# Attention units woven matmul by matmul into the second product of a fused attention and MLP kernel, and the last unit's values moved into the next tile's first blocks

## The chip, the cores and the metric

The kernel runs on one core of one Trainium2 chip. The metric is the device time of one execution in microseconds (us); lower is better. TensorE (PE in the profile) does the matmuls and transposes, VectorE (DVE) and ScalarE (ACT) the element-wise work, GpSimd (POOL) and SyncE (SP) start the transfers.

## The reference

Eight batches of eight heads, 576 positions, head size 64, go through attention with a sliding window of 32 positions to either side. The result, 4608 tokens of 512 features, goes through two matrix products with a tanh-approximated Gelu between them. Inputs and output are float32.

```python
scores = scale * np.matmul(q, k.transpose(0, 1, 3, 2))        # scale = 1/sqrt(64)
mask = np.abs(pos[:, None] - pos[None, :]) <= 32
scores = np.where(mask, scores, -1e9)
attn = softmax(scores)                                        # max taken off, exp, sum
x = (attn @ v).transpose(0, 2, 1, 3).reshape(4608, 512)
h = x @ w_in                                                  # w_in 512 x 2048
g = 0.5 * h * (1 + tanh(sqrt(2/pi) * (h + 0.044715 * h**3)))
out = g @ w_out                                               # w_out 2048 x 512
```

## The kernel before

Everything on TensorE is done in fp16 with float32 accumulation. The tokens of a batch are ordered so that a batch is 576 neighbouring columns of one large tile in SBUF, `xT`, which has the features on the partitions: four groups of 128 features, and group number pr holds the heads 2pr and 2pr+1. The two products work on nine tiles of 512 tokens. Tile t needs columns 512t to 512t+511, so it needs batches up to t, and the attention of batch t+1 is computed while tile t goes through its products. Batch 0 is computed ahead of all tiles (the prologue). Tiles 0 to 6 carry the attention of batches 1 to 7; tiles 7 and 8 carry none.

The first product of tile t, in `ffn_in`, makes 16 blocks of 128 hidden features, each of four accumulating matmuls (`dc` 0 to 3, one for each group of features of `xT`), followed by the Gelu on ACT, which writes into the tile `gT`. The second product, in `ffn_out`, makes four blocks of 128 tokens, each of 16 accumulating matmuls, followed by a copy (`yo`) on DVE and the transfers out. Both kinds of block take their accumulator from one ring of three PSUM buffers (`psM`): a new block has to wait until the block three places earlier has been emptied by its Gelu or its copy.

Attention of a batch comes in eight units: four pairs of heads (pr), two halves of the sequence each. For a unit, `scores` issues six matmuls into the PSUM tile `ps_s`, then an exponential on ACT (`pe`, line 204) and a multiplication with the 0/1 mask on DVE (`pm`, line 206). `values` issues twelve matmuls into `ps_od`, which give the weighted values and the row sums, then a logarithm and an exponential of its negative on ACT (`lt`, line 231, and `rt`, line 233: together the reciprocal of the sums), and a multiplication on DVE that writes the normalised result into `xT` (line 234, "normalisation" below). `ps_s` and `ps_od` have one buffer each. So scores u+1 have to wait for the exponential of unit u, and values u+1 for the normalisation of unit u.

Ahead of the units, q and k have to be cast to fp16 on DVE and transposed on TensorE into `QT` and `KT`: `cast_tail` and `trans_tail` for the last 64 positions of all heads, `cast_pair` and `trans_pair` for the rest of each pair. This is done between the blocks of the first product of tile t for batch t+1. The transposes all go through one PSUM buffer. The loads of q and k for batch t+2 are issued on SP at the start of tile t, behind the output transfers of tile t-1; the loads of v are issued on POOL.

The order is written out by hand: each engine runs its instructions in the order in which the program issues them. In the second product, TensorE's 64 matmuls were cut into 16 runs of four (`ffn_out(t, t4, f0, f1)`), and a table `sched` says which unit calls stand ahead of which run: scores u ahead of run 3u/2 (rounded down), values u two runs later. Ahead of this, `load_exp_table` switches ACT's function table from Gelu to logarithm and exponential; the switch back to Gelu stands ahead of the first Gelu of the next tile.

Of the kernel before, what the change touches and what calls it, by code (L numbers as in the profile page):

```python
# [9 lines left out]
FP32 = mybir.dt.float32  # L10
FP16 = mybir.dt.float16
AF = mybir.ActivationFunctionType
# [12 lines left out]
    1: [(2, 72, 104), (3, 88, 136), (4, 120, 144)],  # L25
}
SW = 416


@with_exitstack  # L30
def kernel(
# [9 lines left out]
    nc = tc.nc  # L41
# [4 lines left out]
    NF = DF // 128  # L46
# [7 lines left out]
    def load_exp_table():  # L54
        nc.scalar.add_instruction(mybir.InstLoadActFuncSet(  # L55
            name=nc.get_next_instruction_name(), act_func_set_id=exp_set, ins=[], outs=[]))
# [8 lines left out]
    psM = ctx.enter_context(tc.tile_pool(name="psM", bufs=3, space=PSUM))  # L65
# [9 lines left out]
    ones = const.tile([128, 64], FP16, name="ones")  # L75
    masks = [const.tile([128, SW], FP16, name=f"mask{h}") for h in range(2)]
    KTs = [const.tile([128, NPAIR, 640], FP16, name=f"KT{i}") for i in range(2)]
    Vs = [const.tile([128, 5, H, 64], FP16, name=f"V{i}") for i in range(2)]
    w_in16 = big.tile([128, 4, DF], FP16, name="w_in16")
    w_out16 = big.tile([128, NF, DM], FP16, name="w_out16")  # L80
# [4 lines left out]
    def load_qk(b, split):  # L85
        qr = rawp.tile([128, H, 256], FP32, name="qr")
        kr = rawp.tile([128, H, 256], FP32, name="kr")
        tr = rawp.tile([128, H, 64], FP32, name="tr")
        raws[b] = (qr, kr, tr)
        step = H // split  # L90
        for h0 in range(0, H, step):
            for src, dst in ((q, qr), (k, kr)):
                nc.sync.dma_start(
                    dst[:, h0:h0 + step, :],
                    src[b, h0:h0 + step, 0:512, :].rearrange("h (p j) d -> p h (j d)", j=4))
            if h0 == 0:
                nc.sync.dma_start(tr[0:64, :, :], q[b, :, 512:576, :].rearrange("h s d -> s h d"))
                nc.sync.dma_start(tr[64:128, :, :], k[b, :, 512:576, :].rearrange("h s d -> s h d"))

    def load_v(b):  # L100
        V = Vs[b % 2]
        for c in range(4):
            nc.gpsimd.dma_start(V[:, c, :, :],  # L103
                                v[b, :, 128 * c:128 * c + 128, :].rearrange("h p d -> p h d"))
        nc.gpsimd.dma_start(V[0:64, 4, :, :], v[b, :, 512:576, :].rearrange("h p d -> p h d"))
# [11 lines left out]
    for h in range(2):  # L117
# [3 lines left out]
        for (c, p0, p1) in PIECES[h]:  # L121
# [11 lines left out]
            off += 4 * n  # L133
        assert off == SW
    for i in range(4):
# [12 lines left out]
    def cast_tail(b):  # L148
        t16 = hp.tile([128, H, 64], FP16, name="t16")
        nc.vector.tensor_copy(t16, raws[b][2])  # L150
        halfs[b] = t16
        QTs[b] = ap_.tile([128, NPAIR, 4, NP_], FP16, name="QT")

    def trans_tail(b):
        t16 = halfs[b]
        pt = psT.tile([128, NPAIR, 128], FP16, name="pt", tag="T", padded_shape=[128, 8, 128])
        for pr in range(NPAIR):
            nc.tensor.transpose(pt[:, pr, :], t16[:, 2 * pr:2 * pr + 2, :], idn)
        for pr in range(NPAIR):
            nc.vector.tensor_copy(  # L160
                QTs[b][:, pr, :, 128:144],
                pt[:, pr, 0:64].rearrange("d (p j) -> d j p", j=4))
        nc.vector.tensor_copy(KTs[b % 2][:, :, 512:576], pt[:, :, 64:128])

    def cast_pair(b, pr):
        qr, kr, tr = raws[b]
        q16 = ap_.tile([128, 4, 2, 64], FP16, name="q16")
        k16 = ap_.tile([128, 4, 2, 64], FP16, name="k16")
        for src, dst in ((qr, q16), (kr, k16)):
            nc.vector.tensor_copy(  # L170
                dst.rearrange("p j h d -> p h j d"),
                src[:, 2 * pr:2 * pr + 2, :].rearrange("p h (j d) -> p h j d", j=4))
        halfs[(b, pr)] = (q16, k16)
# [15 lines left out]
    def scores(b, u):  # L189
# [3 lines left out]
        for (c, p0, p1) in PIECES[hf]:  # L193
# [8 lines left out]
            off += 4 * n  # L202
        pe = ap_.tile([128, 2, SW], FP16, name="pe")
        nc.scalar.activation(pe, ps[:, :, 0:SW], AF.Exp, scale=SCALE)  # L204
        pm = ap_.tile([128, 2, SW], FP16, name="pm")
        nc.vector.tensor_tensor(  # L206
            pm, pe, masks[hf].rearrange("p (o w) -> p o w", o=1).broadcast_to([128, 2, SW]),
            op=ALU.mult)
        units[(b, u)] = pm

    def values(b, u):
        pr, hf = u // 2, u % 2
        pm = units.pop((b, u))
        V = Vs[b % 2]
        od = psO.tile([128, 2, 512], FP32, name="ps_od")
        off = 0
        last = len(PIECES[hf]) - 1
        for i, (c, p0, p1) in enumerate(PIECES[hf]):
            n = p1 - p0
            a, e = p0 - HALF * hf, p1 - HALF * hf  # L220
            for w in range(2):
                for h in range(2):
                    r0 = 64 * h
                    nc.tensor.matmul(  # L224
                        od[r0:r0 + 64, w, 0:4 * HALF].rearrange("d (j p) -> d j p", j=4)[:, :, a:e],
                        V[:, c, 2 * pr + h, :] if w == 0 else ones,
                        pm[:, h, off:off + 4 * n].rearrange("k (j p) -> k j p", j=4),
                        start=(i == 0), stop=(i == last), skip_group_check=True)
            off += 4 * n
        lt = ap_.tile([128, 4 * HALF], FP32, name="lt")  # L230
        nc.scalar.activation(lt, od[:, 1, 0:4 * HALF], AF.Ln)  # L231
        rt = ap_.tile([128, 4 * HALF], FP32, name="rt")
        nc.scalar.activation(rt, lt, AF.Exp, scale=-1.0)  # L233
        nc.vector.tensor_tensor(  # L234
            xT[:, pr, b * S:(b + 1) * S].rearrange("d (j p) -> d j p", j=4)[:, :, HALF * hf:HALF * hf + HALF],
            od[:, 0, 0:4 * HALF].rearrange("d (j p) -> d j p", j=4),
            rt.rearrange("d (j p) -> d j p", j=4), op=ALU.mult)


    gTs = {}  # L240

    def ffn_in(t, fc):
        if fc == 0:
            gTs[t] = gp.tile([128, NF, 512], FP16, name="gT")
        ph = psM.tile([128, 512], FP32, name="ph", tag="mm")
        for dc in range(4):
            nc.tensor.matmul(ph, w_in16[:, dc, fc * 128:fc * 128 + 128],  # L247
                             xT[:, dc, t * 512:(t + 1) * 512],
                             start=(dc == 0), stop=(dc == 3))
        nc.scalar.activation(gTs[t][:, fc, :], ph, AF.Gelu_apprx_tanh)  # L250

    out_v = out.rearrange("(b p j) f -> b j p f", b=B, j=4)
    pys = {}

    def ffn_out(t, t4, f0, f1):
        if f0 == 0:
            pys[t4] = psM.tile([128, 512], FP32, name="py", tag="mm")
        py = pys[t4]
        for fc in range(f0, f1):
            nc.tensor.matmul(py, gTs[t][:, fc, t4 * 128:t4 * 128 + 128], w_out16[:, fc, :],  # L260
                             start=(fc == 0), stop=(fc == NF - 1))
        if f1 == NF:
            yo = yp.tile([128, 512], FP32, name="yo")
            nc.vector.tensor_copy(yo, py)  # L264
            g = t * 512 + t4 * 128
            end = g + 128
            m = 0
            while g < end:
                seg = g // NP_
                e = min(end, (seg + 1) * NP_)  # L270
                p0 = g - seg * NP_
                nc.sync.dma_start(out_v[seg // 4, seg % 4, p0:p0 + e - g, :], yo[m:m + e - g, :])
                m += e - g
                g = e
# [12 lines left out]
    values(0, 7)  # L287


    for t in range(NT):  # L290
        b = t + 1
        att = b < B
        if att and b + 1 < B:
            load_qk(b + 1, 1)
            load_v(b + 1) if b + 1 >= 2 else None
        for fc in range(NF):
            if att:
                if fc == 1:
                    cast_tail(b)
                    cast_pair(b, 0)  # L300
                if fc == 2:
                    trans_tail(b)
                if fc in (4, 7, 10, 13):
                    pr = (fc - 4) // 3
                    trans_pair(b, pr)
                    if pr < 3:
                        cast_pair(b, pr + 1)
            ffn_in(t, fc)
        sched = {}
        if att:  # L310
            load_exp_table()
            for u in range(8):
                sched.setdefault((3 * u) // 2, []).append((scores, u))
                sched.setdefault((3 * u) // 2 + 2, []).append((values, u))
        for i in range(16):
            for fn, u in sched.get(i, []):
                fn(b, u)
            ffn_out(t, i // 4, 4 * (i % 4), 4 * (i % 4) + 4)


# [28 lines left out]
```

## Time and profile before

| | us |
|---|---|
| median of 3 runs | 402.92 (402.8 to 403.68) |
| the profiled execution | 404.22 |
| its span, first to last instruction | 402.5 |
| TensorE busy in it | 337.8 (84%) |
| ACT busy | 213.5 (53%) |
| DVE busy | 156.7 (39%) |
| one stage with attention (second product of a tile, first product of the next) | 42.75 |
| mean granted clock of TensorE | 0.998 of full speed |

In a row of the timeline stand the start and the duration in us, the engine, the source line, the operation, output and inputs by the program's names, the number of instructions, and in brackets how long the engine had been idle before and what ended that. Matmuls overlap in the array, and their ends are modelled, so the distance from one group's start to the next group's start is what a group costs TensorE, and not its duration. A row of the view by stretches has the stretch, its length, then for TensorE, its weight loads, DVE, ACT and POOL the busy time with the number of instructions, then the granted clock, the share of the transfer engines and GB/s. In the table of waits stand the total in us, the number of waits and the longest.

### The profile page before, as it was taken

The page shows a single profiled execution, that of the slowest core. Times are in us where ns is not written, and L with a number is a line of the kernel's source. Part 1 is how long each engine was busy: PE and PEld are TensorE (multiplying, and loading weights), DVE is VectorE, ACT ScalarE, POOL GpSimd, SP SyncE. Part 2 cuts the span into 40 slices and gives each one's busy share as a digit, 9 for nine tenths or more (in the row PEclk, how much of TensorE's full clock was granted, in tenths as well). Part 3 has the DMA queues.
Part 4 walks back from the last instruction along what each step waited for, and adds up shares of the span by engine and source line. Part 5 has one row for each costly group of instructions (what it writes and reads, how often), then busy time and mean ns, then how long its engine had stood idle before and what let it go on. Part 6 is the DMA issues. An engine that isn't in the chain of part 4 may idle for free.

```text
span 402.5 us, 6406 instructions
## 1 busy us (share of the span) xinstructions
PE 337.8 (84%) x2592; PEld 171.4 (43%) x2592; DVE 156.7 (39%) x347; ACT 213.5 (53%) x352; POOL 45.0 (11%) x67
## 2 busy tenths in 40 slices
PE   0454997899789988898889978997899888999995
PEld 0343453445344534454444534453445344444442
DVE  3545443445244524453454434452445244002011
ACT  1254566555755565646555665557555656530710
POOL 9512120040004000400012000400000000000000
PEclk9999999999999999999999999999999999999999
DMA  9999990197029900594019501980110001002102
GB/s 173 265 238 215 252 156 20 36 137 210 2 52 82 267 1 29 66 207 100 28 31 209 135 12 43 126 221 0 54 30 24 2 26 55 26 5 76 28 26 78
DMA packets 72574, 37.64 MB, mean 94 GB/s; under 512 B 47456, under 2 KB 67936, under 8 KB 72544
## 3 DMA queue, kind: packets, MB, share of 16 engines
q1 hardware_dynamic: 30816, 28.32, 25.6%
q0 software_dynamic: 41728, 8.92, 24.5%
q8 instruction: 20, 0.33, 0.4%
q14 instruction: 10, 0.08, 0.1%
HBM read 36.70 MB, written 9.44 MB: 115 GB/s over the span
## 4 chain that ended last, share of the span: by engine, by line
PE 67%; ACT 19%; DVE 6%; issue 4%; POOL 3%; ACTq 0%; POOLq 0%
PE ph L247 31%; PE py L260 20%; PE ps_od L224 9%; ACT pe L204 7%; ACT lt L231 6%; DVE xT L234 4%; ACT rt L233 4%; PE ps_s L197 3%; ACT L55 2%; PE pt L179 2%; PE pt L181 2%; POOL V L103 1%; POOL w_in L116 1%; POOL mask L125 1%; POOL mask L127 0%
## 5 line engine op out<-in xcount | busy, mean ns | idle before, releaser
L260 PE MATMUL py<-w_out,gT 128*128 128x512 f16 x576 | 140.4, 381 | 0.0
L247 PE MATMUL ph<-xT,w_in 128*128 128x512 f16 x576 | 133.6, 383 | 0.1
L250 ACT ACTIVATE gT<-ph 128x512 f16<-128x512 f32 x144 | 86.0, 597 | 80.8 <-PE ph L247 80.8
L247 PEld LDWEIGHTS <-w_in 128*128 128x128 f16 x576 | 55.2, 99 | 60.9 <-issue 2.2
L204 ACT ACTIVATE pe<-ps_s 128x832 f16<-128x832 f32 x64 | 54.8, 857 | 35.2 <-PE ps_s L197 35.1
L260 PEld LDWEIGHTS <-gT 128*128 128x128 f16 x576 | 48.8, 97 | 54.4
L206 DVE TENSOR_TENSOR pm<-pe,mask 128x832 f16<-128x832 f16 x64 | 37.9, 592 | 59.6 <-ACT pe L204 58.2
L234 DVE TENSOR_TENSOR xT<-ps_od,rt 128x288 f16<-128x288 f32 x64 | 29.3, 458 | 66.4 <-ACT rt L233 66.4
L231 ACT ACTIVATE lt<-ps_od 128x288 f32<-128x288 f32 x64 | 26.2, 410 | 52.3 <-PE ps_od L224 52.3
L103 POOL DMA_DIRECT2D V<-in_v_dram x32 | 28.6, 901 | 204.3 <-PE ps_od L224 178.5
L224 PE MATMUL ps_od<-pm,V 128*64 128x192 f16 (+4 forms) x384 | 35.7, 240 | 18.1 <-DVE xT L234 17.9
L264 DVE COPY yo<-py 128x512 f32<-128x512 f32 x36 | 24.7, 686 | 65.0 <-PE py L260 65.0
L197 PE MATMUL ps_s<-QT,KT 64*128 64x192 f16 (+4 forms) x384 | 24.2, 233 | 25.8 <-ACT pe L204 22.0
L224 PEld LDWEIGHTS <-V 128*64 128x64 f16 x384 | 26.1, 115 | 42.3 <-issue 42.2
L224 PE MATMUL ps_od<-pm,ones 128*64 128x192 f16 (+4 forms) x384 | 33.4, 236 | 0.0
L197 PEld LDWEIGHTS <-KT 64*128 64x128 f16 x384 | 14.8, 97 | 42.8 <-issue 36.6
L182 DVE COPY QT<-pt 128x512 f16<-128x512 f16 x32 | 13.6, 425 | 40.7 <-PE pt L181 40.7
L233 ACT ACTIVATE rt<-lt 128x288 f32<-128x288 f32 x64 | 28.3, 442 | 2.0
L179 PE MATMUL pt<-idn,q 128*128 128x128 f16 x128 | 13.3, 230 | 15.4 <-DVE q L170 15.4
L224 PEld LDWEIGHTS <-ones 128*64 128x64 f16 x384 | 25.1, 116 | 0.0
L183 DVE COPY KT<-pt 128x512 f16<-128x512 f16 x32 | 21.8, 681 | 0.0
L179 PEld LDWEIGHTS <-q 128*128 128x128 f16 x128 | 10.0, 102 | 22.4 <-DVE q L170 15.8
(27 smaller groups left out, 106.9 us busy)
## 6 DMA issues: line engine op xcount, KB each, us to landing
qr<-in_q_dram SPq DMA_DIRECT2D x7, 1024.0 KB, 7.3
kr<-in_k_dram SPq DMA_DIRECT2D x7, 1024.0 KB, 10.6
V<-in_v_dram POOLq DMA_DIRECT2D x32, 128.0 KB, 5.2
w_in<-in_moe_w_in_dram POOLq DMA_DIRECT2D x4, 512.0 KB, 22.3
w_out<-in_moe_w_out_dram POOLq DMA_DIRECT2D x4, 512.0 KB, 29.4
out_dram<-yo SPq DMA_DIRECT2D x8, 256.0 KB, 2.4
out_dram<-yo SPq DMA_DIRECT2D x8, 224.0 KB, 2.4
out_dram<-yo SPq DMA_DIRECT2D x8, 192.0 KB, 3.2
```

The source lines that it names most:

```text
L103: nc.gpsimd.dma_start(V[:, c, :, :], v[b, :, 128 * c:128 * c + 128, :].rearrange("h p d -> p h d"))
L179: nc.tensor.transpose(pt[:, j, :], q16[:, j, :, :], idn)
L197: nc.tensor.matmul(ps[:, h, off:off + 4 * n].rearrange("k (j p) -> k j p", j=4), KTs[b % 2][r0:r0 + 64, pr, 128 * c:128 * c + 128], QTs[b] ...
L204: nc.scalar.activation(pe, ps[:, :, 0:SW], AF.Exp, scale=SCALE)
L206: nc.vector.tensor_tensor(pm, pe, masks[hf].rearrange("p (o w) -> p o w", o=1).broadcast_to([128, 2, SW]), op=ALU.mult)
L224: nc.tensor.matmul(od[r0:r0 + 64, w, 0:4 * HALF].rearrange("d (j p) -> d j p", j=4)[:, :, a:e], V[:, c, 2 * pr + h, :] if w == 0 else ones ...
L231: nc.scalar.activation(lt, od[:, 1, 0:4 * HALF], AF.Ln)
L233: nc.scalar.activation(rt, lt, AF.Exp, scale=-1.0)
L234: nc.vector.tensor_tensor(xT[:, pr, b * S:(b + 1) * S].rearrange("d (j p) -> d j p", j=4)[:, :, HALF * hf:HALF * hf + HALF], od[:, 0, 0:4 ...
L247: nc.tensor.matmul(ph, w_in16[:, dc, fc * 128:fc * 128 + 128], xT[:, dc, t * 512:(t + 1) * 512], start=(dc == 0), stop=(dc == 3))
L250: nc.scalar.activation(gTs[t][:, fc, :], ph, AF.Gelu_apprx_tanh)
L260: nc.tensor.matmul(py, gTs[t][:, fc, t4 * 128:t4 * 128 + 128], w_out16[:, fc, :], start=(fc == 0), stop=(fc == NF - 1))
```

## The change

`ffn_out` now issues one matmul, and the second product is a loop over 64 of them. The unit calls have positions in this loop, counted in matmuls: scores 0 ahead of matmul 0, scores u ahead of matmul 15 + 7(u-1) for u from 1 to 7, values u ahead of matmul 19 + 7u for u from 0 to 6. So scores 7 stand ahead of matmul 57, and values 6 ahead of matmul 61. Values u now come behind scores u+1.

Values 7 stand behind the 64th matmul. `ffn_in` can issue part of a block (`d0` to `d1`), and the first three blocks of the next tile are begun here with their first three matmuls, which read the groups of features 0 to 2 of `xT`: block 0 ahead of values 7, blocks 1 and 2 behind them. Group 3 is what units 6 and 7 write. The next tile's loop begins with the three fourth matmuls and their Gelus, and goes on with block 3. All three buffers of the ring are held by these blocks until their Gelus.

The casts and transposes of q and k move by one or two blocks: the tail's casts and transposes and the first pair's cast to block 3 (from blocks 1 and 2), the transposes of the pairs to blocks 5, 8, 11 and 14 (from 4, 7, 10 and 13).

```diff
--- before.py
+++ after.py
@@ -25,6 +25,10 @@
     1: [(2, 72, 104), (3, 88, 136), (4, 120, 144)],
 }
 SW = 416
+
+
+
+FIRST, LAG, STEP = 15, 4, 7
 
 
 @with_exitstack
@@ -238,28 +242,32 @@
 
 
     gTs = {}
-
-    def ffn_in(t, fc):
-        if fc == 0:
+    phs = {}
+
+    def ffn_in(t, fc, d0=0, d1=4):
+        if fc == 0 and d0 == 0:
             gTs[t] = gp.tile([128, NF, 512], FP16, name="gT")
-        ph = psM.tile([128, 512], FP32, name="ph", tag="mm")
-        for dc in range(4):
+        if d0 == 0:
+            phs[fc] = psM.tile([128, 512], FP32, name="ph", tag="mm")
+        ph = phs[fc]
+        for dc in range(d0, d1):
             nc.tensor.matmul(ph, w_in16[:, dc, fc * 128:fc * 128 + 128],
                              xT[:, dc, t * 512:(t + 1) * 512],
                              start=(dc == 0), stop=(dc == 3))
-        nc.scalar.activation(gTs[t][:, fc, :], ph, AF.Gelu_apprx_tanh)
+        if d1 == 4:
+            nc.scalar.activation(gTs[t][:, fc, :], ph, AF.Gelu_apprx_tanh)
 
     out_v = out.rearrange("(b p j) f -> b j p f", b=B, j=4)
     pys = {}
 
-    def ffn_out(t, t4, f0, f1):
-        if f0 == 0:
+    def ffn_out(t, i):
+        t4, fc = i // NF, i % NF
+        if fc == 0:
             pys[t4] = psM.tile([128, 512], FP32, name="py", tag="mm")
         py = pys[t4]
-        for fc in range(f0, f1):
-            nc.tensor.matmul(py, gTs[t][:, fc, t4 * 128:t4 * 128 + 128], w_out16[:, fc, :],
-                             start=(fc == 0), stop=(fc == NF - 1))
-        if f1 == NF:
+        nc.tensor.matmul(py, gTs[t][:, fc, t4 * 128:t4 * 128 + 128], w_out16[:, fc, :],
+                         start=(fc == 0), stop=(fc == NF - 1))
+        if fc == NF - 1:
             yo = yp.tile([128, 512], FP32, name="yo")
             nc.vector.tensor_copy(yo, py)
             g = t * 512 + t4 * 128
@@ -287,35 +295,51 @@
     values(0, 7)
 
 
+    begun = False
     for t in range(NT):
         b = t + 1
         att = b < B
         if att and b + 1 < B:
             load_qk(b + 1, 1)
             load_v(b + 1) if b + 1 >= 2 else None
-        for fc in range(NF):
+        if begun:
+
+            for fc in range(3):
+                ffn_in(t, fc, 3, 4)
+        for fc in range(3 if begun else 0, NF):
             if att:
-                if fc == 1:
+                if fc == 3:
                     cast_tail(b)
                     cast_pair(b, 0)
-                if fc == 2:
                     trans_tail(b)
-                if fc in (4, 7, 10, 13):
-                    pr = (fc - 4) // 3
+                if fc in (5, 8, 11, 14):
+                    pr = (fc - 5) // 3
                     trans_pair(b, pr)
                     if pr < 3:
                         cast_pair(b, pr + 1)
             ffn_in(t, fc)
-        sched = {}
         if att:
             load_exp_table()
+            at = {0: [(scores, 0)]}
             for u in range(8):
-                sched.setdefault((3 * u) // 2, []).append((scores, u))
-                sched.setdefault((3 * u) // 2 + 2, []).append((values, u))
-        for i in range(16):
-            for fn, u in sched.get(i, []):
-                fn(b, u)
-            ffn_out(t, i // 4, 4 * (i % 4), 4 * (i % 4) + 4)
+                if u:
+                    at.setdefault(FIRST + STEP * (u - 1), []).append((scores, u))
+                if u < 7:
+                    at.setdefault(FIRST + LAG + STEP * u, []).append((values, u))
+            for i in range(64):
+                for fn, u in at.pop(i, []):
+                    fn(b, u)
+                ffn_out(t, i)
+            assert not at
+            ffn_in(t + 1, 0, 0, 3)
+            values(b, 7)
+            ffn_in(t + 1, 1, 0, 3)
+            ffn_in(t + 1, 2, 0, 3)
+            begun = True
+        else:
+            for i in range(64):
+                ffn_out(t, i)
+            begun = False
 
 
 # ---- launch: one core; inputs and outputs as the reference has them ----
```

## The prediction

> **What bounds the kernel now.** I read the page first (span, engines), then the table of waits, then one tile's stage in the view by stretches and the timeline. Page and waits (us in total, times, longest):
>
> ```profile
> span 402.5 us, 6406 instructions
> PE 337.8 (84%) x2592; PEld 171.4 (43%) x2592; DVE 156.7 (39%) x347; ACT 213.5 (53%) x352; POOL 45.0 (11%) x67
> ...
> PE ps_s L197 <- ACT pe L204: 22.0, 29, 1.6
> PE ps_od L224 <- DVE xT L234: 17.9, 32, 1.5
> ```
>
> TensorE is the busiest engine, and its large waits are both in the attention units: the next scores wait for the exponential to empty their only score tile, the next values for the normalisation to empty their only output tile. Two stretches of one stage (tile 3: second product with attention, then the first product of tile 4; columns are length, then busy time by engine):
>
> ```profile
> 187.70:214.53 26.83, 21.82 (x209) 10.91 (x209) 10.20 (x19) 16.55 (x27) 4.21 (x5) 1.00 0.28 41
> 214.53:230.45 15.92, 15.92 (x101) 8.19 (x100) 8.61 (x23) 8.96 (x15) 0.00 (x0) 1.00 0.88 185
> ```
>
> The first product keeps TensorE busy for all its 15.92 us; the second, with units in it, lasts 26.83 us of which 21.82 are busy. Together 42.75 us, a stage. Where the idle time sits (timeline: start, duration; in brackets idle time before, and what ended it):
>
> ```profile
> 187.70 0.35 PE L197 MATMUL ps_s<-QT,KT 64*128 64x160 f16 x6
> 187.80 0.60 ACT L250 ACTIVATE gT<-ph 128x512 f16<-128x512 f32 x1 [0.27 <-PE ph L247]
> 187.99 1.04 PE L260 MATMUL py<-w_out,gT 128*128 128x512 f16 x4
> 188.42 1.28 ACT L55 ACT_TABLE_LOAD   x1
> 189.71 0.86 ACT L204 ACTIVATE pe<-ps_s 128x832 f16<-128x832 f32 x1
> 190.63 0.36 PE L197 MATMUL ps_s<-QT,KT 64*128 64x128 f16 x6 [1.60 <-ACT pe L204]
> 190.92 1.04 PE L260 MATMUL py<-w_out,gT 128*128 128x512 f16 x4
> 191.02 0.86 ACT L204 ACTIVATE pe<-ps_s 128x832 f16<-128x832 f32 x1 [0.45 <-PE ps_s L197]
> 191.88 0.26 PE L224 MATMUL ps_od<-pm,V 128*64 128x160 f16 x2
> 191.92 0.59 DVE L206 TENSOR_TENSOR pm<-pe,mask 128x832 f16<-128x832 f16 x1 [0.72 <-ACT pe L204]
> ...
> 192.37 1.04 PE L260 MATMUL py<-w_out,gT 128*128 128x512 f16 x4
> 192.48 0.41 ACT L231 ACTIVATE lt<-ps_od 128x288 f32<-128x288 f32 x1 [0.60 <-PE ps_od L224]
> 192.92 0.44 ACT L233 ACTIVATE rt<-lt 128x288 f32<-128x288 f32 x1
> 193.40 0.46 DVE L234 TENSOR_TENSOR xT<-ps_od,rt 128x288 f16<-128x288 f32 x1 [0.89 <-ACT rt L233]
> 193.91 0.25 PE L224 MATMUL ps_od<-pm,V 128*64 128x128 f16 x2 [0.50 <-DVE xT L234]
> ...
> 196.19 0.36 PE L197 MATMUL ps_s<-QT,KT 64*128 64x128 f16 x6 [0.47 <-ACT pe L204]
> ```
>
> A stage has one wait of 1.60, then 0.47 and 0.50 in turn: two units come close together and then four matmuls of the product are too few to cover either chain. The chain from one unit's values to when the next may start is 193.91 - 191.88 = 2.03 us, and TensorE resumes 0.05 us after DVE ends.
>
> **The change part by part.** Seven tiles (0 to 6) carry attention; the others are untouched. Counts of matmuls, activations, copies, table loads and DMAs stay the same, so only waits and switches can move. Prices on TensorE:
>
> ```profile
> 342.97 13.81 PE ph L247 x64
> ...
> 186.31 1.46 PE L247 MATMUL ph<-xT,w_in 128*128 128x512 f16 x6
> ...
> 181.53 0.39 PE L179 MATMUL pt<-idn,q 128*128 128x128 f16 x4
> 181.98 2.75 PE L247 MATMUL ph<-xT,w_in 128*128 128x512 f16 x12
> ```
>
> (the first row from the chain that ended last, the others from the timeline). A matmul of a product, m, is 13.81/64 = 0.216 us. One scores call is 187.99 - 187.70 = 0.29, one values call 192.37 - 191.88 = 0.49. Entering a unit out of a product costs extra: four matmuls are 0.86, but 190.92 to 191.88 is 0.96; six from 186.31 end at 187.61 and the scores start at 187.70. So an entry, e, is 0.10 for both kinds. The transposes of one pair take 181.98 - 181.53 = 0.45, those of the tail half of that, 0.22.
>
> Work of one stage without any wait, with all 16 units entered out of a product as the new order has it: 128 x 0.2158 = 27.62, scores 8 x 0.29 = 2.32, values 8 x 0.49 = 3.92, entries 1.60, transposes 4 x 0.45 + 0.22 = 2.02; sum 37.48. Against 42.75 this leaves at most 5.27 us to gain per stage.
>
> Now the new order by hand, time 0 at scores 0 of a stage. Scores 0 end at 0.29; 15 matmuls and an entry put scores 1 at 3.63. Their tile is empty when exponential 0 has ended: 190.63 - 187.70 = 2.93. So the wait of 1.60 goes; its cover is 15 matmuls where there were four. Four matmuls later values 0 start at 4.88, three after them scores 2 at 6.12, and from there each unit takes 7m + 2e + 0.29 + 0.49 = 2.49 us. Values need the previous values' 2.03: 0.46 to spare. Scores need the exponential one step earlier, about 0.39 + 0.86 + 0.05 = 1.30: ample. In the step ACT does 0.86 + 0.41 + 0.44 = 1.71. On DVE the copies of finished output blocks (0.69) come between; the one of the third block falls behind normalisation 4 and delays mask 6 by about 0.2, which values 6 need 1.7 us later. So inside the second product I cost waits at nothing; without the cover each would be the old 0.5.
>
> Values 6 start at 19.82, end at 20.31, and three matmuls end the product at 20.96. The tail is where waits come back:
>
> ```profile
> 210.59 0.25 PE L224 MATMUL ps_od<-pm,V 128*64 128x128 f16 x2 [0.50 <-DVE xT L234]
> ...
> 212.08 1.28 ACT L250 ACT_TABLE_LOAD   x1
> ...
> 214.74 0.69 DVE L264 COPY yo<-py 128x512 f32<-128x512 f32 x1 [2.18 <-PE py L260]
> 215.34 0.42 DVE L150 CAST t<-tr 128x512 f16<-128x512 f32 x1
> ...
> 216.69 0.40 SPq L93 DMA_DIRECT2D qr<-in_q_dram  x1
> ```
>
> Block 0's three matmuls end at 21.60, the entry at 21.70, but normalisation 6 is done for TensorE at 19.82 + 2.03 = 21.85: **0.15 wait**. Values 7 run from 21.85 to 22.34. Blocks 1 and 2 (six matmuls) end at 23.64; block 2 takes the buffer of the last output block, whose DVE copy (0.69, queued behind normalisation 6) ends near 22.55, in time. The fourth matmul of block 0 needs normalisation 7, at 21.85 + 2.03 = 23.88: **0.24 wait**. Three fourth matmuls end at 24.53. The tail cast (0.42) runs on DVE right behind normalisation 7 and ends near 24.3, so the tail's transposes go at once, to 24.75. Block 3 then needs the buffer of block 0, which its Gelu must empty. The table load starts 212.08 - 210.59 = 1.49 after values 7, at 23.34, the Gelu 1.29 later at 24.63 (188.42 to 189.71); with 0.60 for it and 0.05 to resume, block 3 starts at 25.28: **0.53 wait**. Behind it are 13 blocks (52m = 11.22), four pairs of transposes (1.80) and an entry: next scores 0 at 38.40. Saved: 42.75 - 38.40 = 4.35 us. The output's DMAs and the q, k, v loads for a later batch keep their order on their queues and come no later in the stage. The loads issued from 216.69 on are used one stage later and land within about 11 us of issue (median of the slowest kind, from the page), so a shorter stage leaves them over 20 us:
>
> ```profile
> kr<-in_k_dram SPq DMA_DIRECT2D x7, 1024.0 KB, 10.6
> ```
>
> The Trainium skill bears on the table load: "ScalarE: Activation LUTs", What ACT_TABLE_LOAD costs, adds a drain of about 1.38 us to each switch of tables. By it block 3 would start 1.38 later, and the estimate would be 9.7 us longer. The rows above contradict it: Gelu ends at 188.40, load at 188.42, exponential at 189.71, with no drain between; I keep 1.29.
>
> **Sum.** Six stages run from scores 0 to the next scores 0: 6 x 4.35 = 26.1. The seventh ends in a tile without attention:
>
> ```profile
> 316.69 1.28 ACT L55
> ```
>
> Its scores 0 stand 0.72 before that load (187.70 against 188.42), at 315.97; its following first product ended at 342.97 + 13.81 = 356.78: 40.81 us. New: 25.28 + 11.22 = 36.50, so 4.3 saved. In all 30.4 us. The profiled execution took 404.22 us (span 402.5 and 1.7 around it), so it would be 373.8; it was 1.3 above the median of the runs, 402.92, so for the runs I take 402.92 - 30.4 = **372.5**.
>
> **Rivals.**
>
> *Cheaper tail.* If the three tail waits (0.92 together) vanish, 7 x 0.92 = 6.4 more is gained: **366.1**. Against: each follows from a row. Chance 0.07.
>
> *Uncovered tail.* The early blocks could be held until normalisation 7, the whole tile xT being awaited and not its columns; then the change doesn't do what it says. Block 0 would start at 21.85, values 7 at 22.60, normalisation 7 be done at 24.63, six and then one matmul end block 0 at 26.14, its Gelu (0.2 after, 0.60, 0.05) free block 3 at 27.0: 1.7 later than forecast, 12 in all, **384.5**. Against it, the prologue:
>
> ```profile
> 41.21 3.83 PE L247 MATMUL ph<-xT,w_in 128*128 128x512 f16 x8
> ...
> 42.23 0.46 DVE L234 TENSOR_TENSOR xT<-ps_od,rt 128x288 f16<-128x288 f32 x1 [1.92 <-ACT rt L233]
> ```
>
> Block 0 of tile 0 began 1.48 us before normalisation 7 ended, so waits follow columns. Chance 0.08.
>
> *Dearer switches.* The pipeline's whole tail might be paid at each entry where none is hidden in a wait: 1.04 - 0.86 = 0.18 and not 0.10 (a block of four against 4m). 16 x 0.08 x 7 = 9 us: **381.5**. Against: unstalled entries, at 191.88 and 187.70, cost 0.10. Chance 0.07. The Trainium skill, "TensorEngine Tiling (Array Packing)", Tiling Modes, says that changing the tiling mode drains TensorE, which is this rival's ground and speaks against single-matmul interleaving; the trace bears out a cost, of 0.10.
>
> *A full round trip per unit: slower.* In the new order exponential u+1 stands ahead of logarithm u on ACT, and mask u+1 ahead of normalisation u on DVE. If values u can finish only after unit u+1's chain, a step is scores to mask (190.63 to 191.92 + 0.59: 1.88) plus 2.03, 3.91 us in place of 2.49. Six steps: +8.5, less 4.35, +4.2 a stage, +29: **432**. It turns slower from a step of 2.49 + 4.35/6 = 3.2. For it: both orders are in the queues. Against: logarithm 0 starts 0.60 after values 0 with an exponential just before it, and ACT's 1.71 fits in 2.49. Chance 0.03.
>
> *Nothing gained*: the q and k loads set the stage after all and take back the whole, 402.9. They would have to land some 25 us later than they do; chance 0.01.
>
> **How the numbers follow.** My forecast, 372.5 within about 369 to 377, has 0.74. The range 366 to 382 takes in the cheaper tail and the dearer switches and leaves out the uncovered tail and the slower cases. A difference of 0.2% (0.8 us) is about what runs of this kernel can tell from none; faster by more 0.96, within it 0.01, slower 0.03.
>
> **What would show it.** Right: no idle time before scores and values inside the second product; values 2.49 us apart; stages of 38.4; idle time only in the tail, before values 7 (0.15), block 0's fourth matmul (0.24) and block 3 (0.53, ended by Gelu). Wrong: blocks 1 and 2 starting after normalisation 7, seven matmuls with two entries over 1.71 us, waits for mask or normalisation in mid-product, transposes of the tail waiting for their cast, or a granted clock below 1.00.

## The result, and the profile after

The changed kernel takes 373.19 us (median; 372.62 to 374.80) against 403.05 us before (402.8 to 403.68) on the same chip: a ratio of 0.926, 95% interval 0.923 to 0.929. The profiled execution took 373.34 us, its span is 371.6. First the page of the changed kernel, and from its table of waits (total us, times, longest) the three rows of TensorE that bear on units and blocks:

```profile
span 371.6 us, 6392 instructions
PE 338.2 (91%) x2592; PEld 164.6 (44%) x2592; DVE 156.8 (42%) x347; ACT 214.4 (58%) x352; POOL 45.6 (12%) x67
...
PE ps_od L228 <- DVE xT L238: 3.9, 4, 1.5
PE ph L254 <- ACT gT L258: 3.1, 7, 0.8
PE ps_s L201 <- ACT pe L208: 1.0, 1, 1.0
```

The busy times are those of before; the idle time of TensorE is what went. Waits of scores for the exponential fell from 22.0 us in 29 places to 1.0 us in one, those of values for the normalisation from 17.9 in 32 to 3.9 in 4, and all five that are left lie in the prologue. Seven waits are new: one in each stage, for a Gelu. The table counts only what lies between the modelled end of one group and the start of the next, so a wait shorter than the overlap of the matmuls is not in it; such waits are read from the distances of starts. The view by stretches, cut where the last matmul of the second product has been issued and where the next scores 0 stand:

```profile
174.04:195.10 21.06, 21.06 (x198) 9.62 (x198) 9.25 (x17) 14.49 (x24) 0.66 (x1) 1.00 0.15 39
195.10:212.45 17.35, 16.83 (x115) 8.58 (x113) 9.70 (x25) 11.14 (x19) 3.82 (x5) 1.00 1.10 187
```

A stage is 38.41 us where it was 42.75. In the second product TensorE is busy for all of 21.06 us; the 0.5 us that the view leaves idle lie in the tail. The start of that second product in the timeline:

```profile
174.04 0.35 PE L201 MATMUL ps_s<-QT,KT 64*128 64x160 f16 x6
174.32 3.41 PE L268 MATMUL py<-w_out,gT 128*128 128x512 f16 x15
176.05 0.86 ACT L208 ACTIVATE pe<-ps_s 128x832 f16<-128x832 f32 x1
177.67 0.35 PE L201 MATMUL ps_s<-QT,KT 64*128 64x128 f16 x6
177.95 1.04 PE L268 MATMUL py<-w_out,gT 128*128 128x512 f16 x4
178.92 0.26 PE L228 MATMUL ps_od<-pm,V 128*64 128x160 f16 x2
...
180.16 0.35 PE L201 MATMUL ps_s<-QT,KT 64*128 64x160 f16 x6
...
181.41 0.25 PE L228 MATMUL ps_od<-pm,V 128*64 128x128 f16 x2
```

No row has an idle time in brackets: exponential 0 has ended at 176.91 when scores 1 start at 177.67, where before they waited 1.60. The units stand 2.49 us apart (178.92 to 181.41). The end of the same second product and the begun blocks:

```profile
193.88 0.26 PE L228 MATMUL ps_od<-pm,V 128*64 128x160 f16 x2
...
195.03 0.81 PE L254 MATMUL ph<-xT,w_in 128*128 128x512 f16 x3
...
195.91 0.25 PE L228 MATMUL ps_od<-pm,V 128*64 128x128 f16 x2
...
196.39 2.34 PE L254 MATMUL ph<-xT,w_in 128*128 128x512 f16 x9
...
197.40 1.28 ACT L258 ACT_TABLE_LOAD   x1
197.41 0.46 DVE L238 TENSOR_TENSOR xT<-ps_od,rt 128x288 f16<-128x288 f32 x1 [0.96 <-ACT rt L237]
...
198.57 0.39 PE L162 MATMUL pt<-idn,t 128*128 128x128 f16 x4
198.69 2.31 ACT L258 ACTIVATE gT<-ph 128x512 f16<-128x512 f32 x4
...
199.34 1.89 PE L254 MATMUL ph<-xT,w_in 128*128 128x512 f16 x8 [0.39 <-ACT gT L258]
```

Block 0's three matmuls and an entry (0.65 and 0.10) would put values 7 at 195.78; they start at 195.91, after 0.13 us of waiting. Nine matmuls at 0.2158 us would end at 198.33; the tail's transposes follow at 198.57, so 0.24 us of waiting are hidden in that merged row. The transposes cost 0.22, and block 3, at 199.34, has waited 0.55 (0.39 by the bracket, which counts from the modelled end) for the first Gelu, which could not start before the table load had ended.

### The profile page after: what moved, and what is told of

Its sections match the earlier page's. It is cut to its first block, busy times and chain, and to the rows that moved or that the text cites. A ratio compares the mean times of both kernels' runs of the same rounds, so it can differ in the third digit from the quotient of the medians.

```text
span 371.6 us, 6392 instructions
## 1 busy us (share of the span) xinstructions
PE 338.2 (91%) x2592; PEld 164.6 (44%) x2592; DVE 156.8 (42%) x347; ACT 214.4 (58%) x352; POOL 45.6 (12%) x67
## 2 busy tenths in 40 slices
DMA packets 72574, 37.64 MB, mean 101 GB/s; under 512 B 47456, under 2 KB 67936, under 8 KB 72544
## 4 chain that ended last, share of the span: by engine, by line
PE 82%; ACT 9%; DVE 4%; POOL 3%; issue 1%; POOLq 0%
PE py L268 35%; PE ph L254 29%; PE ps_od L228 9%; PE ps_s L201 5%; ACT rt L237 3%; ACT lt L235 2%; ACT L258 2%; PE pt L185 2%; PE pt L183 2%; DVE xT L238 2%; ACT gT L258 1%; POOL V L107 1%; POOL w_in L120 1%; ACT pe L208 1%; POOL mask L129 1%
## 5 line engine op out<-in xcount | busy, mean ns | idle before, releaser
L268 PE MATMUL py<-w_out,gT 128*128 128x512 f16 x576 | 142.9, 381 | 0.0
L254 PE MATMUL ph<-xT,w_in 128*128 128x512 f16 x576 | 135.3, 382 | 3.6 <-ACT gT L258 3.1
L258 ACT ACTIVATE gT<-ph 128x512 f16<-128x512 f32 x144 | 84.5, 597 | 58.5 <-PE ph L254 57.5
L208 ACT ACTIVATE pe<-ps_s 128x832 f16<-128x832 f32 x64 | 55.2, 862 | 37.5 <-PE ps_s L201 37.4
L268 PEld LDWEIGHTS <-gT 128*128 128x128 f16 x576 | 47.7, 98 | 51.9
L228 PEld LDWEIGHTS <-V 128*64 128x64 f16 x384 | 23.4, 115 | 29.5 <-issue 29.1
L186 DVE COPY QT<-pt 128x512 f16<-128x512 f16 x32 | 13.6, 425 | 43.1 <-PE pt L185 43.1
L201 PEld LDWEIGHTS <-KT 64*128 64x128 f16 x384 | 12.3, 97 | 29.8 <-issue 25.0
L228 PEld LDWEIGHTS <-ones 128*64 128x64 f16 x384 | 24.0, 117 | 0.0
## 6 DMA issues: line engine op xcount, KB each, us to landing
kr<-in_k_dram SPq DMA_DIRECT2D x7, 1024.0 KB, 13.6
```

The lines of the kernel that those rows point to most:

```text
L201: nc.tensor.matmul(ps[:, h, off:off + 4 * n].rearrange("k (j p) -> k j p", j=4), KTs[b % 2][r0:r0 + 64, pr, 128 * c:128 * c + 128], QTs[b] ...
L228: nc.tensor.matmul(od[r0:r0 + 64, w, 0:4 * HALF].rearrange("d (j p) -> d j p", j=4)[:, :, a:e], V[:, c, 2 * pr + h, :] if w == 0 else ones ...
```

## The experiments

The theory is that of the prediction: the gain is the waits between units, which a longer cover removes; what is left is the tail and the price of leaving the product. Runs 1 to 4 share one chip (before: 403.93 us there), runs 5 to 7 share one (before: 404.07).

### 1 and 2: each half of the change alone

Only the weaving; values 7 at the end of the second product, no block begun early:

```diff
-            ffn_in(t + 1, 0, 0, 3)
             values(b, 7)
-            ffn_in(t + 1, 1, 0, 3)
-            ffn_in(t + 1, 2, 0, 3)
-            begun = True
+            begun = False
```

> Second product woven matmul by matmul as in the changed kernel, but no block of the next tile is begun early: values 7 stand behind the last matmul and block 0 follows whole. Theory (the two unit chains and the tail as worked out in the prediction): normalisation 6 holds values 7 back by 0.79 us, normalisation 7 holds the fourth matmul of block 0 back by 0.9, block 3 no longer waits for a Gelu; a stage is 0.76 longer than in the changed kernel, 7 x 0.76 = 5.3: about 378.5. Rival (the gain came from moving the last unit's values, the finer order alone gives little): above 390.

Measured: 378.0 us (ratio to before 0.936, 0.933 to 0.939). The theory's 378.5 holds and the rival's 390 does not: a stage is 39.15 us, 0.74 longer than in the changed kernel. Its tail in the timeline has the two waits that it named, for normalisation 6 and for normalisation 7 (0.78 and 0.88 by the distances of starts, 0.71 each from the modelled ends):

```profile
159.49 0.25 PE L228 MATMUL ps_od<-pm,V 128*64 128x128 f16 x2 [0.71 <-DVE xT L238]
...
161.51 2.10 PE L254 MATMUL ph<-xT,w_in 128*128 128x512 f16 x9 [0.71 <-DVE xT L238]
```

Only the early blocks; the units at their old places, counted in matmuls:

```diff
-            at = {0: [(scores, 0)]}
+            at = {}
             for u in range(8):
-                if u:
-                    at.setdefault(FIRST + STEP * (u - 1), []).append((scores, u))
+                at.setdefault(4 * ((3 * u) // 2), []).append((scores, u))
                 if u < 7:
-                    at.setdefault(FIRST + LAG + STEP * u, []).append((values, u))
+                    at.setdefault(4 * ((3 * u) // 2 + 2), []).append((values, u))
```

> Units stay at their old places ahead of runs of four matmuls; only values 7 move into the first blocks of the next tile, as in the changed kernel. Theory: the waits of 1.60, 0.47 and 0.50 stay; only the last 0.50 goes and tail waits of about 0.25 and 0.05 come; block 3 starts 0.66 us earlier in a stage, 7 x 0.66 = 4.6: about 398.4 with 403.05 before. Rival (the move of the last unit is what counts): 380 or less.

Measured: 405.19 us, a ratio of 1.003 (1.002 to 1.005): slightly slower than before, and a miss of 6.8 us. The rival, 380 or less, is refuted too. The count was wrong:

```profile
209.13 4.49 PE L268 MATMUL py<-w_out,gT 128*128 128x512 f16 x20
...
213.46 0.81 PE L254 MATMUL ph<-xT,w_in 128*128 128x512 f16 x3
...
214.20 0.25 PE L228 MATMUL ps_od<-pm,V 128*64 128x128 f16 x2
```

Behind values 6 stand 20 matmuls and not the 16 that I had counted; four more are 0.86 us, 6.0 in seven stages, and with them the expected 398.4 becomes 404.4, or 405.3 on this chip; a stage is 42.96 us where before it was 42.75, and 42.75 - 0.66 + 0.86 is 42.95. This leaves nothing for the casts and transposes of q and k, which stand at their new blocks in this run too. Moving the last unit alone gives nothing, because in the old order 16 matmuls already stood behind values 7 and covered all that follows them. Woven, the same move gives about 4.5 us (378.0 against 373.53 in run 5, on a chip with nearly the same time before). The weaving alone is worth 403.93 - 378.0 = 25.9 of the 30. It does two things, the finer cut and the even spacing; units spaced evenly between runs of four matmuls were not tried, so whether the finer cut is needed stays open. Run 6 shows that it is not enough.

### 3: the price of leaving the product

```diff
-            for u in range(8):
-                if u:
-                    at.setdefault(FIRST + STEP * (u - 1), []).append((scores, u))
-                if u < 7:
-                    at.setdefault(FIRST + LAG + STEP * u, []).append((values, u))
+            for u in range(7):
+                at[FIRST + STEP * u] = [(scores, u + 1), (values, u)]
```

> As the changed kernel, but values u stand directly behind scores u+1, at the same matmul (15 + 7u), so the product is left for units 9 times a stage and not 16. Theory (an entry out of a product costs 0.10, values behind scores cost none): seven entries less, 0.70, and the wait of 0.15 before values 7 gone; 7 x 0.85 = 6.0: about 367.2. Rival (each change of the tiling of the array costs alike, so a change between scores and values costs as much as one out of the product): only the 0.15 goes, about 372.

Measured: 367.45 us (ratio 0.909, 0.907 to 0.911). A stage is 37.53 us (37.55 by the theory). Its timeline:

```profile
175.95 0.35 PE L201 MATMUL ps_s<-QT,KT 64*128 64x128 f16 x6
176.24 0.26 PE L228 MATMUL ps_od<-pm,V 128*64 128x160 f16 x2
...
176.72 1.69 PE L268 MATMUL py<-w_out,gT 128*128 128x512 f16 x7
...
178.34 0.35 PE L201 MATMUL ps_s<-QT,KT 64*128 64x160 f16 x6
```

Scores still cost 0.29, values 0.48, and only one entry of 0.10 is left: seven matmuls (1.51) take 178.34 - 176.72 = 1.62. So a step is 2.39 and not 2.49. The rival as I put it is refuted, but it had been put badly: with one price for every change of tiling, the changes around a pair of calls fall from four to three, which saves the same 0.1. What the 0.29 and 0.49 hold points that way. Scores stream 416 columns through each half of the array, and the two halves must overlap, since one after the other they would take 832/512 x 0.2158 = 0.35. By an estimate at the product's price per column they take 416/512 x 0.2158 = 0.175 side by side; values, with twice as many, 0.351. Between 0.11 and 0.14 is left in each, which an exit could explain. That every change costs about 0.1 is thus likely but not shown. The Trainium skill, "TensorEngine Tiling (Array Packing)", Tiling Modes, gives a drain at every change of mode, without a price. The 0.10 of an entry agrees with it; that a drain is what costs it was not tested.

### 4: no tail waits

Units six matmuls apart, the first at 13; values 7 inside the second product; no block begun early:

```diff
-FIRST, LAG, STEP = 15, 4, 7
+FIRST, LAG, STEP = 13, 4, 6
...
-                if u < 7:
-                    at.setdefault(FIRST + LAG + STEP * u, []).append((values, u))
+                at.setdefault(FIRST + LAG + STEP * u, []).append((values, u))
...
-            ffn_in(t + 1, 0, 0, 3)
-            values(b, 7)
-            ffn_in(t + 1, 1, 0, 3)
-            ffn_in(t + 1, 2, 0, 3)
-            begun = True
+            begun = False
```

> Units six matmuls apart and two matmuls earlier (scores u ahead of matmul 13 + 6(u-1), values u ahead of 17 + 6u, values 7 ahead of matmul 59), no block begun early. Theory: a step is 6m + 0.98 = 2.28 us, above the 2.03 of the values chain, so no wait comes in mid-product; behind values 7 stand 5 matmuls and whole blocks, which cover normalisation 7, the table load and the first Gelu, so all three tail waits (0.93 together) go: a stage is 37.5, about 366.7. Rival (ACT or DVE cannot keep a step of 2.28, or the tail waits were not what held the stage): 372 or more.

Measured: 368.07 us (ratio 0.911, 0.908 to 0.914), 1.4 above the expectation; the rival is refuted. A stage is 37.64 us and not 37.5, which makes 1.0 of the 1.4. The timeline behind values 6 (189.54):

```profile
189.54 0.26 PE L228 MATMUL ps_od<-pm,V 128*64 128x160 f16 x2
...
191.56 0.25 PE L228 MATMUL ps_od<-pm,V 128*64 128x128 f16 x2
...
192.05 1.25 PE L268 MATMUL py<-w_out,gT 128*128 128x512 f16 x5
193.14 2.75 PE L254 MATMUL ph<-xT,w_in 128*128 128x512 f16 x12
195.73 0.39 PE L162 MATMUL pt<-idn,t 128*128 128x128 f16 x4
195.95 1.89 PE L254 MATMUL ph<-xT,w_in 128*128 128x512 f16 x8
```

From 193.14 blocks 0 to 2, the transposes and block 3 follow without a gap: 12 x 0.2158 = 2.59 to 195.73. The three tail waits were real, and 17 matmuls behind the last unit, where the changed kernel has nine ahead of the transposes, hide them. The 0.14 that a stage is too long is a small wait that I had overlooked: between values 6 and 7 no scores stand, so their distance would be 6m + 0.10 + 0.49 = 1.88, below the floor of 2.03, and the rows show 2.02.

### 5: the changed kernel once more

> The changed kernel as it is, beside the other runs on this chip. Theory: 373 to 374 with 403 to 404 before; stages of 38.4 us.

Measured: 373.53 us (ratio 0.924, 0.922 to 0.927).

### 6: the floor of a step

```diff
-FIRST, LAG, STEP = 15, 4, 7
+FIRST, LAG, STEP = 15, 2, 3
```

> As the changed kernel, but units three matmuls apart, values two matmuls behind the scores (scores u ahead of matmul 15 + 3(u-1), values u ahead of 17 + 3u for u to 6). The same work in another order. Theory (the floor of a step is the chain from values to the next values, 2.03 us): a step of 3m + 0.98 = 1.63 is too short, values wait about 0.4 each, a step is 2.03, and the rest of the product stands behind the units; a stage of 40.7, about 2.3 longer than in the changed kernel, 16 in all: about 389. Rival (no such floor, any cover will do): 372. Rival (scores, exponential, mask and the values chain in one round trip of 3.9): above 450.

Measured: 389.59 us (ratio 0.964, 0.962 to 0.967), a stage of 40.67. The timeline has the wait for the normalisation at each unit:

```profile
187.61 0.25 PE L228 MATMUL ps_od<-pm,V 128*64 128x128 f16 x2 [0.38 <-DVE xT L238]
...
189.63 0.26 PE L228 MATMUL ps_od<-pm,V 128*64 128x160 f16 x2 [0.32 <-DVE xT L238]
...
191.65 0.25 PE L228 MATMUL ps_od<-pm,V 128*64 128x128 f16 x2 [0.32 <-DVE xT L238]
```

A step is 2.02 us: the floor is the chain from values to the next values, and neither a round trip of 3.9 nor nothing. It costs 16 us although every matmul is the same: matmuls saved between the units stand uselessly behind them.

### 7: both gains together

```diff
-FIRST, LAG, STEP = 15, 4, 7
+FIRST, LAG, STEP = 13, 4, 7
...
-            for fc in range(3):
+            for fc in range(2):
                 ffn_in(t, fc, 3, 4)
-        for fc in range(3 if begun else 0, NF):
+        for fc in range(2 if begun else 0, NF):
...
-            for u in range(8):
-                if u:
-                    at.setdefault(FIRST + STEP * (u - 1), []).append((scores, u))
-                if u < 7:
-                    at.setdefault(FIRST + LAG + STEP * u, []).append((values, u))
+            for u in range(7):
+                at[FIRST + STEP * u] = [(scores, u + 1), (values, u)]
+            at[63] = [(values, 7)]
...
-            values(b, 7)
             ffn_in(t + 1, 1, 0, 3)
-            ffn_in(t + 1, 2, 0, 3)
```

> The two gains together: values u directly behind scores u+1 at matmul 13 + 7u, values 7 ahead of the last matmul, only blocks 0 and 1 of the next tile begun early. Theory: seven entries less (0.70) and nearly all of the tail waits (0.93) gone, with about 0.15 of small waits put in for the first mask and normalisations 6 and 7: a stage of 36.9, 10.5 us less than the changed kernel: about 363. Rival (the two gains overlap): about 367.

Measured: 363.98 us (ratio to before 0.900, 0.897 to 0.903), the fastest version, 9.6 us less than the changed kernel beside it. From the view by stretches, four stages long:

```profile
150.00:300.00 150.00, 149.98 (x1253) 75.69 (x1247) 76.79 (x171) 100.87 (x171) 13.12 (x15) 1.00 0.45 90
```

The view shows no idle time of TensorE in the stages, which are 37.01 us long. The two gains nearly add: 38.41 less 0.70 and 0.93 would be 36.78, so 0.23 us a stage was given back in small waits that the overlap hides, and not 0.15. They lie here:

```profile
174.38 0.36 PE L201 MATMUL ps_s<-QT,KT 64*128 64x128 f16 x6
174.73 0.26 PE L228 MATMUL ps_od<-pm,V 128*64 128x160 f16 x2
...
192.09 2.93 PE L254 MATMUL ph<-xT,w_in 128*128 128x512 f16 x12
193.26 0.68 DVE L272 COPY yo<-py 128x512 f32<-128x512 f32 x1
...
194.86 0.39 PE L162 MATMUL pt<-idn,t 128*128 128x128 f16 x4
```

Values 0 start 0.35 behind scores 1 and not 0.29, and the twelve matmuls from 192.09 take 2.77 and not 2.59. The 0.18 fits block 2, which needs the buffer of the last output block, and that is free only when its copy ends at 193.94; the expectation had put this wait down to normalisations 6 and 7.

## Why the prediction was right

It gave 372.5 within 366 to 382; measured 373.19. By its own steps, in us from scores 0 of a stage (174.04 in the trace after):

| step | predicted | measured |
|---|---|---|
| scores 1 | 3.63 | 177.67: 3.63 |
| values 0 | 4.88 | 178.92: 4.88 |
| distance of units | 2.49 | 2.49 |
| values 6 | 19.82 | 193.88: 19.84 |
| block 0 begun | 20.96 | 195.03: 20.99 |
| values 7, after a wait for normalisation 6 | 21.85 | 195.91: 21.87 |
| tail's transposes | 24.53 | 198.57: 24.53 |
| block 3, after a wait for a Gelu | 25.28 | 199.34: 25.30 |
| next scores 0 (stage) | 38.40 | 38.41 |

The prices taken from the trace of before (m, an entry, scores, values, the values chain) carried over unchanged to a different order, since each had been read as a distance between starts, with the switch in it. The one small term that did not come inside the second product is the delay of mask 6 by 0.2: it starts at 191.43, when exponential 6 has ended at 191.39.

The rivals. *Cheaper tail*: no, all three waits came, with 0.13, 0.24 and 0.55 for 0.15, 0.24 and 0.53; run 4 shows that they can be ordered away. *Uncovered tail*: no; blocks 1 and 2 start at 196.39, ahead of normalisation 7 (197.41 to 197.87). *Dearer switches*: no; a block of four and an entry take 178.92 - 177.95 = 0.97 without any wait. *Full round trip*: no; the step is 2.49, and 2.02 where the cover is cut away. *Nothing gained* by late loads: no wait for a load is among the new ones, although these landed later than before (13.6 us for k, before 10.6):

```profile
kr<-in_k_dram SPq DMA_DIRECT2D x7, 1024.0 KB, 13.6
```

The table load: 197.40 plus 1.28 is 198.68, and the Gelu starts at 198.69. The drain of 1.38 that the Trainium skill states ("ScalarE: Activation LUTs", What ACT_TABLE_LOAD costs) is not there; by it block 3 would have started near 200.7.

Two terms were mis-sized. The seventh stage saved 4.12 (from scores 0 at 289.25 to the end of the next first product at 325.94, 36.69) and not 4.31. These ends stand in the chain, before and after:

```profile
356.78 13.81 PE py L260 x64
325.94 13.81 PE py L268 x64
```

The chain goes by modelled ends. In the timeline the same products start 0.16 earlier, at 356.62 and 325.78. The prediction took its 36.50 from starts, which is right (325.78 - 289.25 = 36.53), and set it against 40.81, which ends at a modelled end; by starts the stage of before is 40.65. And the profiled execution of before lay 1.3 above its median, which I took off; that of the changed kernel lies at its median (373.34 against 373.19). Of the 30.9 us between the two profiled executions 6 x 4.34 = 26.0 and 4.1 are the stages, and 0.6 came ahead of them, with scores 0 of the first tile at 58.81 and not 59.44. These 0.6 may be chance: in the second profile of the changed kernel, which the last section shows, they stand at 59.41.

## What to carry to other kernels

Where small units with single buffers are woven into a long product, write down for each buffer the chain from one use to the next, and space the units so that the work between them is longer than the longest chain: 2.03 us here, with 2.49 of work between. More distance is no use (a step of 2.28 in run 4 has no such wait either), and less costs the full difference per unit. Put the last unit early enough that its chain, and any table switch behind it, is covered by the product that it stands in; and put calls that change the array's tiling side by side, since each way out of the product has a price, 0.10 us here.

## What the runs showed of the hardware

I had not expected TensorE's first product to begin at half rate. The same kernel, twice, from the timeline; the changed kernel's profile first:

```profile
41.34 4.30 PE L254 MATMUL ph<-xT,w_in 128*128 128x512 f16 x12
45.49 0.39 PE L162 MATMUL pt<-idn,t 128*128 128x128 f16 x4
```

and its second profile, run 5:

```profile
40.83 5.41 PE L254 MATMUL ph<-xT,w_in 128*128 128x512 f16 x12
46.08 0.39 PE L162 MATMUL pt<-idn,t 128*128 128x128 f16 x4
```

The weight loads of run 5 show the spacing of the single matmuls:

```profile
43.17 0.15 PEld L254 LDWEIGHTS <-w_in 128*128 128x128 f16 x1 [0.28 <-issue]
43.60 0.15 PEld L254 LDWEIGHTS <-w_in 128*128 128x128 f16 x1 [0.28 <-issue]
```

Twelve matmuls of 0.2158 are 2.59 us; the fourth waits for normalisation 7 of the prologue, some 0.3. They took 4.15 and 5.25, because the first of them stand 0.43 apart, twice m, and the change to 0.216 came soon after 44.1 in the one and between 45.7 and 46.1 in the other. The units of the prologue were slow as well: its values 7 take 0.83 in the first profile (40.51 to 41.34), where values 7 of a stage take 0.48. The view by stretches of the changed kernel's first profile gives a granted clock of 1.00 there all the same:

```profile
41.34:45.49 4.15, 4.08 (x15) 1.47 (x14) 1.46 (x4) 3.33 (x5) 0.88 (x1) 1.00 1.17 247
```

This is 1.1 us in one stretch between two executions of one kernel. The second had begun the stretch 0.5 earlier, so 0.6 of it is left in the spans (371.6 and 372.2). The Trainium skill, "TensorE: Matmul & The Clock Gate", Part 1, describes such a start: half clock until a free-running window of about 3.4 us has been busy. The doubled spacing and the changing moment agree with it; that the window is their cause was not tested.
